# A fused attention and GLU block, forward and backward: GLU LayerNorms moved by one iteration, eight fold products of the backward moved into dQ's bank, start of the backward reordered

## The chip, the cores and the metric

The kernel runs on one core of one Trainium2 chip. The time is the device time of one execution in microseconds (us). A core has five engines that run side by side, each in its own program order: TensorE (PE in the profile, with its weight loads as PEld), VectorE (DVE), ScalarE (ACT), GpSimd (POOL) and SyncE (SP, which here only issues transfers). POOL and ACT issue transfers too. All transfers are carried out by 16 DMA engines. Matrix products write into PSUM, and ACT or DVE copy the results out ("evacuation").

## The reference

One block with two residual branches, and the gradients of all its inputs (cut to what matters):

```python
sa, ca, ga, sb, cb, gb = mod                    # six vectors from silu(c) @ w_mod
h = layernorm(x) * (1 + ca) + sa                # x: 1 x 2048 x 512
x = x + ga * A(h)                               # attention over segments with a memory
h = layernorm(x) * (1 + cb) + sb
x = x + gb * ((sigmoid(h @ w_gate) * (h @ w_up)) @ w_down)     # w_gate, w_up: 512 x 1792

def A(x):                                       # 64 segments of 32 rows, 32 heads of 128
    for s in range(64):
        h = concat([mem, x[32 * s:32 * s + 32]])          # mem: 8 rows, so 40 rows
        q, k, v = h @ Wq, h @ Wk, h @ Wv                  # per head
        p = softmax(where(mask, q @ k.T * scale, -1e9))
        o = (p @ v) @ Wo
        mem = o[:8]                                       # goes on to the next segment
        outs.append(o[8:])

out, vjp = jax.vjp(block, x, mem0, Wq, Wk, Wv, Wo, w_gate, w_up, w_down, c, w_mod)
return out, *vjp(grad_out)
```

Segments hang together through `mem`, forward from first to last, and in the gradient from last to first.

## The kernel before

The work has phases, one after the other: a preparation, the 64 forward segments (phase 2, to about 980 us of the span), the GLU forward and backward (phase 3, 980 to 1318) with its weight gradients (to 1490), the 64 backward segments (phase 4, 1490 to 2479), and the gradients of the attention's weights (phase 5, to the end).

**Phase 2's end.** The probabilities of a segment are transposed on PE and stored in `Pst` by `turn_p` (L872): a copy of rows 96 to 127 and a product with `rden` on rows 0 to 119. For the last segment both are on DVE, in three pieces.

**Phase 3, the GLU.** 16 tiles of 128 rows pass through seven stages, `s0` to `s6`, in a software pipeline of 22 iterations (`run_pipeline`). In iteration `it`, stage k works on tile `it - k`, the deepest stage first, so that `s0` is the last of an iteration. After the stages, `after(it)` runs what else is due.
- `s0(j)` issues the loads of tile j + 1 on SP (four of AOA, then x and grad_out) and makes tile j's residual and LayerNorm: L1150 to L1173, nearly all on DVE; a power on POOL gives `rstd` (L1161), ACT copies the normalised rows to bf16 as `xh2` (L1166, "xh" in the profile, needed in the LayerNorm's backward). Its results are `h2` ("h") and `db`, the gradient of the GLU's output.
- `s1(j)` transposes `h2` and `db` into `hdT` with two DMA transposes on SP (L1183, L1184). Tile 0's LayerNorm and `hdT` are made in phase 2.
- `s2(j)` multiplies by w_gate and w_up (L1205, L1209): 4 groups each of 4 matmuls into 5 PSUM buffers that ACT empties as `sg` (sigmoid, L1206) and `u`. Afterwards DVE makes `hh` and `umh` (L1213, L1215).
- `s3(j)` multiplies `db` by w_down's transpose (L1234); DVE makes `du` and `dg`; SP transposes `hh`, `du` and `dg` (L1227, L1252, L1253), for `s4` to `s6`, which end in L1249 and L1274, the LayerNorm's backward and the stores.

The weights' transposes are made on PE as well, in pieces that `turns` hangs on iterations 2 to 4. `wdT_piece(c)` (L1120) makes two groups of seven transposes of w_down and evacuates each (128 x 896): the first on DVE, the second on ACT. `wT_piece` does the like for w_gate and w_up (L1114, evacuated on ACT, "Wq"). The weights, gradients and transposed weights lie in memory that phases 2 and 4 use under the names Wk, Wv and Wq, and the profile shows those names. PE's and ACT's order is pinned as written up to iteration 2, DVE's order for all of the phase.

**Phase 4, the start.** `ptiles` makes tiles and clears them on POOL (L1562): `dS`, `dOst`, `dKT`, `dQT`, `Qst`, `Kst`. DVE clears `dOT` (L1567). Then SP loads the rows of the last segments, and `proj_b`, twice, multiplies the gradients' rows by Wo's transpose and evacuates them into `RBd`, on ACT and on DVE. `turn_b` transposes RBd, `to_heads` copies the 8 tail rows of each head into dOT on POOL, `dO_tails` (L1675) copies rows of RBd into rows 96 to 119 of `dOst` with three DMAs of POOL (L1678), and one DMA stores zeros of dS as the first gradient of `mem` (L1681). The first `g_ps` product of the first step (L1748) reads dOst.

**Phase 4, a step.** For each segment, `dht` collects the gradient of the segment's input through V's and K's weights in the bank `dh_ps` (128 x 512, four groups of 32 rows that are still to be added). `fold_split` writes it as two bf16 tiles, hi (ACT, L312) and lo (DVE, L313), into the tile dST. `dht_pairs` makes Q's part in a bank `dhq_ps` of 128 x 256 with 16 quads of matmuls (L223), and `split_pair` splits that bank into `dh_hi` (ACT, L230) and `dh_lo` (DVE, L232). `tail.chunk()` then issues some of the products for the 24 or 16 matmuls of the tail rows (`dh_tps`), in all but the first four steps. `fold_sum` (L323) adds it all up: eight products of `dST` with `foldsel`, four of `dh_hi` and four of `dh_lo` with `foldhalf`, into `dh_ft`. ACT copies 8 of its columns into `dyT` (L1866) of the next segment, with which the next step's first products on PE begin. Within phase 4's loop every engine's order is pinned as written.

Of the kernel before, what the change touches and what calls it, by code (L numbers as in the profile page):

```python
# [9 lines left out]
AF = mybir.ActivationFunctionType  # L10
# [30 lines left out]
class K:  # L41
# [395 lines left out]
    def phase2(self):  # L437
        nc, tc, cfg, io = self.nc, self.tc, self.cfg, self.io
        D, DC, H, E, L, M, T, G, NS = cfg.D, cfg.DC, cfg.H, cfg.E, cfg.L, cfg.M, cfg.T, cfg.G, cfg.NS
        GW = 128  # L440
        NP = 3
        PG = 4
# [10 lines left out]
        with ExitStack() as ctx:  # L453
# [39 lines left out]
            NT = cfg.NT  # L493
# [309 lines left out]
            for s in range(NS):  # L803
# [67 lines left out]

                def turn_p(pi):  # L872
                    ps, n = transposes_part(ET, pi)
                    nc.vector.tensor_copy(Pst[96:128, pi * PG:pi * PG + n, :], ps[96:128])
                    nc.vector.tensor_tensor(Pst[0:120, pi * PG:pi * PG + n, :], ps[0:120],
                                            rden[:, pi * PG:pi * PG + n].unsqueeze(2).to_broadcast([120, n, 128]), op=ALU.mult)

# [199 lines left out]
    def phase3(self):  # L1077
# [9 lines left out]
        with ExitStack() as ctx:  # L1087
# [29 lines left out]
                                  tp[:, 0:m * DC, :].rearrange("p (i c) d -> p i (c d)", i=m))  # L1117
                return f

            def wdT_piece(c):  # L1120
                def f():
                    for f0 in range(0, FC, 7):
                        tp = tp8()
                        for i in range(7):
                            nc.tensor.transpose(tp[:, i, :], w_down[:, f0 + i, c * 128:(c + 1) * 128], self.ident[:])
                        self.evac("act" if f0 else "dve", w_downT[:, c, f0 * 128:(f0 + 7) * 128],
                                  tp[:, 0:7, :].rearrange("p i f -> p (i f)"))
                return f

            turns = {2: [wdT_piece(c) for c in range(DC)] + [wT_piece(w_gate, w_gateT, 0, 4, None)],  # L1130
                     3: [wT_piece(w_gate, w_gateT, 4, 10, None), wT_piece(w_up, w_upT, 0, 4, None)],
                     4: [wT_piece(w_up, w_upT, 4, 10, None)]}

# [7 lines left out]
            def s0(j):  # L1141
                r0, r1 = j * 128, (j + 1) * 128
                load(j + 1)
                st = ins.pop(j)
                if j == 0:
                    st.update(x1=self.first_x1, rstd=self.first_st[:, 9:10], xh2=self.first_xh2)
                    return st
                a_rows = st["a_rows"]
                t0 = sbp.tile([128, D], F32, name="t0", tag="f32tmp", bufs=5)
                nc.vector.tensor_tensor(t0[:], a_rows[:], ga_bc[:], op=ALU.mult)  # L1150
                x1 = sbp.tile([128, D], F32, name="x1", bufs=4)
                nc.vector.tensor_tensor(x1[:], t0[:], st["x0"][:], op=ALU.add)
# [12 lines left out]
                nc.vector.tensor_scalar(xhf[:], x1[:], mv[:, 0:1], rstd[:, 0:1], op0=ALU.subtract, op1=ALU.mult)  # L1165
                nc.scalar.activation(xh2[:], xhf[:], AF.Copy)  # L1166
# [3 lines left out]
                nc.vector.tensor_tensor(h2[:], h2a[:], sb_bc[:], op=ALU.add)  # L1170
                nc.gpsimd.dma_start(self.H2ROWS[r0:r1, :], h2[:])
                db = sbp.tile([128, D], BF16, name="db", bufs=2)
                nc.vector.tensor_tensor(db[:], st["dout"][:], gb_bc[:], op=ALU.mult)  # L1173
                nc.gpsimd.dma_start(self.DBROWS[r0:r1, :], db[:])
                st.update(db=db, x1=x1, rstd=rstd, xh2=xh2, h2=h2)
                return st

            def s1(j, st):
                if j == 0:
                    st["hdT"] = self.first_hdT  # L1180
                    return st
                hdT = sbp.tile([128, 2 * DC, 128], BF16, name="hdT", bufs=2)
                nc.sync.dma_start(hdT[:, 0:DC, :], st["h2"][:], transpose=True)  # L1183
                nc.sync.dma_start(hdT[:, DC:2 * DC, :], st["db"][:], transpose=True)  # L1184
                st["hdT"] = hdT
                return st
# [7 lines left out]
            def s2(j, st):  # L1194
# [23 lines left out]
                st.update(sg=sg, hh=hh, umh=umh)  # L1218
                if j == NT - 1:
                    last_hh.append(hh)  # L1220
                return st

            def s3(j, st):
# [151 lines left out]
                if it >= 5:  # L1375
                    later(it)

            self.run_pipeline(NT, [s0, s1, s2, s3, s4, s5, s6], deepest_first=True, after=after)
            self.pin(i0, [ET.DVE])
            self.pin_behind(i0, self.pinned, [ET.PE, ET.DVE, ET.Activation, ET.Pool, ET.SP])  # L1380
            accs = self.flat(self.Wk, 2 * DC * F, 2 * D, F32)
# [148 lines left out]
    def phase4(self):  # L1530
# [7 lines left out]
        with self.p4_ctx as ctx:  # L1538
# [29 lines left out]
            RAd = pt.tile([128, 8 * 128], BF16, name="RAd")  # L1568
            RBds = [pt.tile([128, 8 * 128], BF16, name=f"RBd{i}") for i in range(2)]
            btd = pt.tile([128, 8, 128], BF16, name="btd")  # L1570
            dSs = ptiles("dS", 1)
            dSTs = ptiles("dST", 1, zero=False)
            dOst_t = ptiles("dOst", 1)[0]
            dXTs = {nm: ptiles(nm, n, zero=nm != "dVT") for nm, n in (("dVT", 1), ("dKT", 1), ("dQT", 1))}

            def part3(t, pi):
                return t[:, pi * PW:min((pi + 1) * PW, G * GW)].rearrange("p (g x) -> p g x", x=GW)
# [91 lines left out]
            get_loads(NS - 1)  # L1669
            for hf in range(2):  # L1670
                proj_b(NS // 4 - 1, hf)()()
            turn_b(NS // 4 - 1)()
            to_heads("pool", btd[:], 0, 8, 32, 8, 24)

            def dO_tails(s):  # L1675
                for j in range(3):
                    o = 32 * j + 8 * (s % 4)
                    nc.gpsimd.dma_start(dOst_t[96 + 8 * j:104 + 8 * j, 0:1024], RBds[(s // 4) % 2][o:o + 8, :])  # L1678

            dO_tails(NS - 1)  # L1680
            nc.gpsimd.dma_start(self.DHA[NS, 0:M, :], dSs[0][0:M, 0:D])  # L1681
            nseg_t = 128 // T
            row_stores = []

# [7 lines left out]
            for s in reversed(range(NS)):  # L1692
# [88 lines left out]
                def dht_pairs(X, WT):  # L1781
                    ps = psp.tile([128, 256], F32, name="dhq_ps", tag="p")
                    off = lambda h: (h // 3) * GW + (h % 3) * 32
                    for n in range(H // 2):
                        hs = (2 * n, 2 * n + 1)
                        self.pair_mm(ps, [X[:, off(h):off(h) + 32] for h in hs], [WT[:, h, :] for h in hs], n, H // 2)
                    return ps

                for a, n, eng in ((0, 4, "dve"), (4, 2, "act"), (6, 2, "act")):
# [71 lines left out]
                if split:  # L1861
                    self.pop_later()
                store_rows_x(2)
                ft = self.fold_sum(psp, parts, "dh", "p", pair)
                if dyT_next is not None:
                    nc.scalar.activation(dyT_next[:, :, 0:M], ft[:, :, 0:M], AF.Copy)  # L1866
                g = s // 4
# [428 lines left out]
```

## Time and profile before

| what | us |
|---|---|
| runs: median of 3 (lowest, highest) | 3049.66 (3047.43, 3052.71) |
| profiled execution | 3048.13 |
| its span | 3046.3 |
| busy: PE, DVE, ACT, POOL | 2965.3, 1604.1, 1286.8, 1220.3 |
| granted TensorE clock, mean | 0.993 |
| one step of phase 4 | about 15 |
| one iteration of phase 3, in its middle | 18.8 |

The span runs from the first to the last instruction that the profile holds; times of events below are counted from its start. In lists of events, a row has the start, the duration, the engine, the line of the kernel, the operation, what it writes and reads with the shapes, how many in a row are gathered in it, and in brackets the idle time of the engine just before it with what ended that idle time. "SPq" is SP's queue of transfers; "PEld" a weight load, which runs beside PE's products. Where a row gathers several instructions, its duration goes from the first one's start to the last one's end. Matmuls overlap, so that the price of one is read from start to start.

### The profile page before, as it was taken

Reading aid. Unit: us, or ns where it says so; the run is one execution under the profiler, and the core shown is the slowest. Engines: PE = TensorE matmul, PEld = TensorE weight load, DVE = VectorE, ACT = ScalarE, POOL = GpSimd, SP = SyncE. Lnnn points to the kernel's source line nnn. Section 1 sums busy time; section 2 is a strip of 40 time slices with the busy share of each in tenths; the row PEclk is TensorE's granted clock in tenths of the full one; section 3 lists DMA queues with packets and bytes.
Section 4 is the critical chain, followed back from the end, with each engine's and each line's share of the span. In section 5 each row is a group of like instructions: output and inputs, shape, how many; then the busy total and the mean of one; then the engine's idle time right before and its main releaser. Section 6 shows DMA issues by size and latency. Waiting matters only on the chain.

```text
span 3046.3 us, 106520 instructions
## 1 busy us (share of the span) xinstructions
PE 2965.3 (97%) x44223; PEld 1858.1 (61%) x44297; DVE 1604.1 (53%) x3744; ACT 1286.8 (42%) x3182; POOL 1220.3 (40%) x2645
## 2 busy tenths in 40 slices
PE   6999999999998999999899999999999999999999
PEld 3666666666665544446577777777777754445454
DVE  5656656656655788723355555555555532222221
ACT  2555555555554544312355555555555521101111
POOL 2555555555555222211344444444444422333321
PEclk8999999999999999999999999999999999999999
DMA  9888888888889899987699999999999997666574
GB/s 303 219 224 203 210 220 213 211 213 217 214 209 277 197 232 228 234 267 256 193 249 246 245 244 245 247 248 245 245 247 248 246 288 255 220 196 219 176 241 148
DMA packets 838439, 703.44 MB, mean 231 GB/s; under 512 B 538722, under 2 KB 710914, under 8 KB 837060
## 3 DMA queue, kind: packets, MB, share of 16 engines
q1 hardware_dynamic: 710852, 485.11, 64.0%
q0 software_dynamic: 54512, 148.63, 15.5%
q10 hardware_dynamic: 72592, 62.89, 6.6%
q8 instruction: 348, 5.70, 0.8%
q14 instruction: 135, 1.11, 0.1%
HBM read 295.09 MB, written 276.35 MB: 188 GB/s over the span
## 4 chain that ended last, share of the span: by engine, by line
PE 44%; issue 4%; DMA 1%; POOL 1%; SPq 0%; DVE 0%; ACT 0%; ACTq 0%; POOLq 0%
PE gps L2086 9%; PE dh_ps L215 8%; PE g_ps L1748 6%; PE pass_ps L255 5%; PE gps5o L2100 4%; PE dhq_ps L223 4%; PE dh_tps L215 3%; PE dp_ps L1725 2%; PE tps L1658 2%; PE dp_ps L1733 1%; PE turn_ps L1612 1%; PE dh_ft L323 1%; POOL out_dram L2090 1%; DMA rows<-DVR 1%; DMA rows<-OSR 0%
## 5 line engine op out<-in xcount | busy, mean ns | idle before, releaser
L2086 PE MATMUL gps<-rows,hrows 128*128 128x512 bf16 (+2 forms) x2124 | 415.6, 355 | 1.9
L2086 PEld LDWEIGHTS <-hrows 128*128 128x128 bf16 x2160 | 211.2, 98 | 204.6
L61 ACT ACTIVATE ot<-gps 128x512 bf16<-128x512 f32 (+3 forms) x75 | 41.3, 551 | 376.7 <-PE gps L2086 224.8
L1792 POOL COPY dOst<-RAd 96x512 bf16<-96x512 bf16 x128 | 75.3, 611 | 307.1 <-DVE RAd L63 306.6
L63 DVE CAST ot<-gps 128x512 bf16<-128x512 f32 (+3 forms) x76 | 48.2, 634 | 277.8 <-PE gps L2086 194.4
L658 PE MATMUL pass_ps<-Wv,hT 128*32 128x512 bf16 (+2 forms) x2304 | 188.2, 357 | 0.0
L2090 POOL DMA_DIRECT2D out_dram<-ot x108 | 81.4, 753 | 261.1 <-DVE ot L63 134.3
L255 PEld LDWEIGHTS <-hT 128*32 128x32 bf16 x4096 | 125.2, 97 | 94.4 <-DMA Wq<-in_A_Wq_dram 4.5
L1034 POOL TENSOR_TENSOR Pst<-Pst,rden 120x1408 bf16<-120x1408 bf16 x63 | 159.8, 2536 | 50.2 <-issue 33.8
L61 ACT ACTIVATE dVT<-g_ps 128x480 bf16<-128x480 f32 (+1 forms) x192 | 104.7, 545 | 95.4 <-PE g_ps L1748 95.1
L63 DVE CAST Vst<-pass_ps 96x512 bf16<-96x512 f32 x128 | 87.3, 682 | 106.4 <-ACT RBv L61 101.5
L215 PE MATMUL dh_ps<-WvT,dVT 128*32 128x512 bf16 x2048 | 133.4, 380 | 0.1
L255 PE MATMUL pass_ps<-Wq,hT 128*32 128x512 bf16 x2048 | 125.6, 383 | 4.3 <-DMA Wq<-in_A_Wq_dram 4.3
L2100 PE MATMUL gps5o<-WoT,rows 128*128 128x512 bf16 x580 | 127.8, 379 | 1.0 <-DMA rows<-OSR 0.3
L223 PE MATMUL at_ps<-Wo,OT 128*32 128x256 bf16 x4096 | 125.4, 275 | 3.0 <-DMA Wo<-in_A_Wo_dram 2.6
L658 PE MATMUL pass_ps<-Wv,hb 128*32 128x512 bf16 (+2 forms) x636 | 127.2, 345 | 0.0
L255 PE MATMUL pass_ps<-Wk,hT 128*32 128x512 bf16 x2048 | 125.2, 382 | 1.7 <-POOL hT L547 1.1
L255 PE MATMUL pass_ps<-WoT,dyT 128*32 128x256 bf16 (+1 forms) x3072 | 122.4, 308 | 0.9 <-ACT dyT L1866 0.9
L793 POOL DMA_DIRECT2D Vst<-RBv x192 | 99.2, 522 | 59.4 <-ACT ET L840 38.5
L223 PE MATMUL dhq_ps<-WqT,dQT 128*32 128x256 bf16 x4096 | 122.9, 273 | 0.0
L215 PE MATMUL dh_ps<-WkT,dKT 128*32 128x512 bf16 x2048 | 122.3, 380 | 0.0
L223 PEld LDWEIGHTS <-dQT 128*32 128x32 bf16 x4096 | 109.9, 97 | 15.5
(450 smaller groups left out, 6988.1 us busy)
## 6 DMA issues: line engine op xcount, KB each, us to landing
OSR<-Ost SPq DMA_DIRECT2D x64, 352.0 KB
OT<-OT SPq DMA_DIRECT2D x64, 352.0 KB
VT<-VTr SPq DMA_DIRECT2D x64, 352.0 KB
PS<-Pst SPq DMA_DIRECT2D x64, 352.0 KB
OT_l<-OT SPq DMA_DIRECT2D x64, 352.0 KB
Pst_l<-PS SPq DMA_DIRECT2D x64, 352.0 KB
VT_l<-VT SPq DMA_DIRECT2D x64, 352.0 KB
DVR<-rows_x POOLq DMA_DIRECT2D x64, 352.0 KB, 5.8
```

Source lines behind the costliest of these rows:

```text
L61: return nc.scalar.activation(out, in_, AF.Copy)
L63: return nc.vector.tensor_copy(out, in_)
L215: self.nc.tensor.matmul(ps[32 * j:32 * j + 32, :], lhsT=lhsT, rhs=w, start=(n < 4), stop=(n >= total - 4), tile_position=(0, 32 * j))
L223: nc.tensor.matmul(ps[32 * j:32 * j + 32, :], lhsT=x[k], rhs=w[k][:, 256 * d:256 * d + 256], start=(n == 0), stop=(n == total - 1), tile_p ...
L255: self.nc.tensor.matmul(ps[32 * j:32 * j + 32, :], lhsT=lhs(c), rhs=rhs, start=(c == 0), stop=(c == DC - 1), tile_position=(0, 32 * j))
L658: nc.tensor.matmul(ps[32 * j:32 * j + 32, o * E:(o + n) * E], lhsT=lhsT, rhs=wc[:, 3 * a + hl:3 * (a + n - 1) + hl + 1:3, :], start=(c == ...
L793: nc.gpsimd.dma_start(Vst[96 + 8 * j:104 + 8 * j, :], rb[32 * j + o:32 * j + o + 8, :])
L1034: nc.gpsimd.tensor_tensor(Pst[0:120, :, :], Pst[0:120, :, :], rden[:, :].unsqueeze(2).to_broadcast([120, G, 128]), op=ALU.mult)
L1748: nc.tensor.matmul(ps[:, j, 0:w], lhsT=lh[:, g * GW:(g + 1) * GW], rhs=rh[:, g * GW:g * GW + w], start=True, stop=True)
L2086: nc.tensor.matmul(ps[:, 0:ng * E], lhsT=hrows[:, tp_, c * 128:(c + 1) * 128], rhs=rows[:, tp_, 0:ng * E], start=(tp_ == 0), stop=(tp_ == ...
L2090: nc.gpsimd.dma_start(outw[c * 128:(c + 1) * 128, h0:h0 + 3 * (ng - 1) + 1:3, :], ot[:, 0:ng * E].rearrange("p (h e) -> p h e", e=E))
L2100: nc.tensor.matmul(pss[gg][:], lhsT=src[0][:, src[1], gg * E:(gg + 1) * E], rhs=dyrows[:, tp_, :], start=(tp_ == order[0]), stop=(tp_ == o ...
```

## The change

```diff
 def turn_p(pi):
-    nc.vector.tensor_copy(Pst[96:128, pi * PG:pi * PG + n, :], ps[96:128])
+    nc.scalar.activation(Pst[96:128, pi * PG:pi * PG + n, :], ps[96:128], AF.Copy)
...
-def wdT_piece(c):
-    def f():
-        for f0 in range(0, FC, 7):
+def wdT_pieces():
+    for f0 in range(0, FC, 7):
+        for c in range(DC):
             tp = tp8()
             for i in range(7):
                 nc.tensor.transpose(tp[:, i, :], w_down[:, f0 + i, c * 128:(c + 1) * 128], self.ident[:])
-            self.evac("act" if f0 else "dve", w_downT[:, c, f0 * 128:(f0 + 7) * 128],
+            self.evac("dve" if f0 else "act", w_downT[:, c, f0 * 128:(f0 + 7) * 128],
                       tp[:, 0:7, :].rearrange("p i f -> p (i f)"))
-turns = {2: [wdT_piece(c) for c in range(DC)] + [wT_piece(w_gate, w_gateT, 0, 4, None)],
+turns = {2: [wT_piece(w_gate, w_gateT, 0, 4, None)],
...
 # s0(j)
-nc.scalar.activation(xh2[:], xhf[:], AF.Copy)
+if j == 1:
+    nc.gpsimd.tensor_copy(xh2[:], xhf[:])
+else:
+    nc.scalar.activation(xh2[:], xhf[:], AF.Copy)
...
 # s1(j)
+if j == 1:
+    tp = tp8()
+    for i in range(2 * DC):
+        src = st["h2"] if i < DC else st["db"]
+        nc.tensor.transpose(tp[:, i, :], src[:, (i % DC) * 128:(i % DC) * 128 + 128], self.ident[:])
+    nc.scalar.activation(hdT[:], tp[:], AF.Copy)
+    st["hdT"] = hdT
+    return st
...
 # end of s2(j)
+if j == 0:
+    wdT_pieces()
...
-self.run_pipeline(NT, [s0, s1, s2, s3, s4, s5, s6], deepest_first=True, after=after)
+first = lambda j: s0(j) if j < 2 else None
+second = lambda j, st: s1(j, st if j < 2 else s0(j))
+self.run_pipeline(NT, [first, second, s2, s3, s4, s5, s6], deepest_first=True, after=after)
...
 # phase 4, before the loop
-dSs = ptiles("dS", 1)
+dSs = ptiles("dS", 1, zero=False)
-dOst_t = ptiles("dOst", 1)[0]
-dXTs = {nm: ptiles(nm, n, zero=nm != "dVT") for nm, n in (("dVT", 1), ("dKT", 1), ("dQT", 1))}
+dOst_t = ptiles("dOst", 1, zero=False)[0]
+nc.vector.memset(dOst_t[:], 0.0)
+dXTs = {nm: ptiles(nm, n, zero=False) for nm, n in (("dVT", 1), ("dKT", 1), ("dQT", 1))}
+nc.vector.memset(dSs[0][0:32, 0:D], 0.0)
+for t in (dSs[0], dXTs["dKT"][0], dXTs["dQT"][0]):
+    nc.vector.memset(t[:].rearrange("p (g x) -> p g x", x=GW)[:, :, 120:GW], 0.0)
...
-turn_b(NS // 4 - 1)()
-to_heads("pool", btd[:], 0, 8, 32, 8, 24)
...
+i0 = len(self.traced())
 dO_tails(NS - 1)
+turn_b(NS // 4 - 1)()
+to_heads("pool", btd[:], 0, 8, 32, 8, 24)
 nc.gpsimd.dma_start(self.DHA[NS, 0:M, :], dSs[0][0:M, 0:D])
+self.pin(i0, [mybir.EngineType.Pool])
...
 # dht_pairs, every step of phase 4
-    self.pair_mm(ps, [...], [...], n, H // 2)
+    self.pair_mm(ps, [...], [...], n, H // 2 + 1)
+self.pair_mm(ps, [self.foldsel[:, :]] * 2, parts, H // 2, H // 2 + 1)
...
-ft = self.fold_sum(psp, parts, "dh", "p", pair)
+ft = self.sum_pair(psp, pair, "dh", "p")
```

In words:
- At phase 2's end, the copies of 32 rows go to ACT.
- In phase 3 the LayerNorm of tiles 2 to 15 is made one iteration later, directly before `s1` of the same tile. Tiles 0 and 1 keep their place. Tile 1's `xh2` is copied on POOL, and its `hdT` is made by eight transposes on PE and one copy on ACT, in place of two DMA transposes. The eight groups of w_down's transposes come directly after tile 0's `s2`, the first four evacuated on ACT, the last four on DVE.
- At phase 4's start, POOL clears only Qst and Kst. DVE clears dOst, and of dS, dKT and dQT only the pad columns (120 to 127 of each of 11 groups), and of dS also the rows that are stored as zeros. The three DMAs of `dO_tails` come first on POOL, and POOL's order there is pinned.
- In each step, hi and lo of V's and K's bank are no longer folded by eight products of `fold_sum`. One more quad of `pair_mm`, with `foldsel` as the weights, adds them into Q's bank before that one is split, and `sum_pair` (unchanged; it was used elsewhere) makes the eight remaining products:

```python
def sum_pair(self, psp, parts, name, tag):
    ft = psp.tile([128, self.cfg.DC, 32], F32, name=name + "_ft", tag=tag)
    for i in range(2):
        for c in range(self.cfg.DC):
            self.nc.tensor.matmul(ft[:, c, :], lhsT=parts[i][:, (c % 2) * 128:(c % 2) * 128 + 128],
                                  rhs=self.foldhalf[:, c // 2, :], start=(i == 0 and c == 0), stop=(i == 1),
                                  skip_group_check=True)
    return ft
```

More of the change, by code (lines that the diff above doesn't have):

```diff
@@ L1125, in f @@
                             nc.tensor.transpose(tp[:, i, :], w_down[:, f0 + i, c * 128:(c + 1) * 128], self.ident[:])
-                        self.evac("act" if f0 else "dve", w_downT[:, c, f0 * 128:(f0 + 7) * 128],
+                        self.evac("dve" if f0 else "act", w_downT[:, c, f0 * 128:(f0 + 7) * 128],
                                   tp[:, 0:7, :].rearrange("p i f -> p (i f)"))
-                return f
-            turns = {2: [wdT_piece(c) for c in range(DC)] + [wT_piece(w_gate, w_gateT, 0, 4, None)],
+            turns = {2: [wT_piece(w_gate, w_gateT, 0, 4, None)],
                      3: [wT_piece(w_gate, w_gateT, 4, 10, None), wT_piece(w_up, w_upT, 0, 4, None)],
@@ L1785, in dht_pairs @@
                         hs = (2 * n, 2 * n + 1)
-                        self.pair_mm(ps, [X[:, off(h):off(h) + 32] for h in hs], [WT[:, h, :] for h in hs], n, H // 2)
+                        self.pair_mm(ps, [X[:, off(h):off(h) + 32] for h in hs], [WT[:, h, :] for h in hs], n, H // 2 + 1)
+                    self.pair_mm(ps, [self.foldsel[:, :]] * 2, parts, H // 2, H // 2 + 1)
                     return ps
```

## The prediction

> **What bounds the kernel now.** I read the page's first part, then windows of the places the diff touches, then the timeline of each, and last the waits of PE in the stretches that repeat. Page and windows (columns of a window: us; busy and instruction count of PE, PEld, DVE, ACT, POOL; granted clock; DMA share; GB/s):
>
> ```profile
> PE 2965.3 (97%) x44223; PEld 1858.1 (61%) x44297; DVE 1604.1 (53%) x3744; ACT 1286.8 (42%) x3182; POOL 1220.3 (40%) x2645
> ...
> 988.00:1004.00 16.00, 13.68 (x104) 8.75 (x103) 11.76 (x21) 9.08 (x14) 3.36 (x6) 0.79 0.61 173
> 1004.00:1290.00 286.00, 279.46 (x1503) 137.36 (x1517) 232.87 (x420) 118.75 (x201) 68.19 (x125) 1.00 0.96 224
> 1490.00:1505.00 15.00, 6.95 (x110) 3.87 (x108) 5.28 (x13) 2.71 (x9) 12.18 (x17) 0.85 0.63 202
> 1565.00:2455.00 890.00, 888.48 (x18606) 635.91 (x18610) 516.92 (x1304) 471.38 (x1217) 415.50 (x1027) 1.00 1.00 246
> ```
>
> PE (TensorE) is the bound: 888.48 of 890 us in the backward steps, 279.46 of 286 in the GLU's repeating part, at clock 1.00. So time is won in two ways: fewer PE instructions in those stretches, or the holes at the GLU's start (clock 0.79) and at the backward's start (PE 6.95 of 15, clock 0.85).
>
> **Part 1, the GLU's start.** Timeline (start, duration, engine, line, operation, idle before it and its releaser):
>
> ```profile
> 986.74 0.63 ACT L1166 ACTIVATE xh<-xhf 128x512 bf16<-128x512 f32 x1 [9.85 <-DVE xhf L1165]
> 987.28 0.53 ACT L1206 ACTIVATE sg<-mm 128x448 bf16<-128x448 f32 x1
> 987.86 1.07 PE L1209 MATMUL mm<-Wk,Wq 128*128 128x448 bf16 x4 [4.28 <-ACT sg L1206]
> ...
> 994.45 0.55 PE L1125 MATMUL tp<-ident,Wv 128*128 128x128 bf16 x7 [1.70 <-ACT w_downT L61]
> ...
> 1003.31 0.92 PE L1205 MATMUL mm<-Wk,hdT 128*128 128x448 bf16 x4
> ```
>
> ACT runs in order: tile 1's xh waits for its LayerNorm on DVE and stands ahead of tile 0's first sigmoid, so PE, with its five PSUM buffers full, idles 4.28 us; the clock then reads 0.62, 0.53 (988 to 992). Next, LayerNorm 2 occupies DVE from 989.16 to 994.98, ahead of its w_downT copies. s2(1), PE's next long block, starts at 1003.31.
>
> After: xh(1) is on POOL, so ACT is free. PE fills five buffers by 979.63 + 5 x 0.757 (one L1205 group) = 983.4. The first evacuations must outwait the stores that last read sg's and u's memory. I put the second of these at 984.8, where SP issues a request that waits on the same lane. PE then idles about 1 us and s2(0) ends near 986.8 instead of 991.71. Up to s2(1) PE has 64 transposes (56 of w_down, 8 added for hdT(1)), 7 of them 0.46 apart: 4.2 us; 16 of w_gate, 0.9; 16 matmuls L1234 of 0.19, 3.05. That gives 995.0. With 0.6 for the chain of eight copies (four on ACT at 0.92, four on DVE at 0.62) and hdT's own (1.0): 995.6, 7.7 us earlier. LayerNorm 2 (5.8 us) now stands on DVE behind hh, du, dg of tile 0, as LayerNorm 3 does before: there dg ends at 1005.60 and ACT's Wq copies, queued behind the LayerNorm's xh, come at 1010.71, 5.1 later. After, dg ends 7.7 earlier at best, nearer 6.4 as DVE first makes four of the w_downT copies: 1004.3 for the Wq copies. So 6.4 remain, and **I take 6.2**. Lower bound 4 (stores land 1 us later, one more 1 us copy wait); upper 8.5 (7.7, plus the 0.72 that PE waits for ACT's Wq at 1011.78). POOL's copy of xh(1) has no row: between L1792's 0.61 and L1034's 2.5. It is needed only in tile 1's backward, over 30 us on; its cost is nothing, and at 2.5 it would delay only the H2ROWS store.
>
> The same move in each later tile: LayerNorm keeps its slot on DVE, but hdT's two transposes now follow it at once, and on SP stand behind AOA, x and DAOT and ahead of duT, dgT, hhT.
>
> ```profile
> 1107.34 0.38 SPq L1325 DMA_DIRECT2D DAOT<-daT  x1
> 1108.95 1.72 SPq L1252 DMA_TRANSPOSE duT<-du  x1
> ...
> 1107.89 0.69 DVE L1170 TENSOR_TENSOR h<-h2a,Wv 128x512 bf16<-128x512 f32 x1
> ...
> 1117.82 0.92 PE L1205 MATMUL mm<-Wk,hdT 128*128 128x448 bf16 x4
> ...
> 1109.00:1110.00 1.00, 1.00 (x6) 0.46 (x5) 1.00 (x2) 0.00 (x0) 0.97 (x2) 1.00 0.08 16
> ```
>
> h is ready at 1108.58; hdT(h) takes SP 1.2 to 1.3, so it is issued by 1109.9 and needed by s2 at 1117.82: 7.9 us, where it had 16. The db half is needed only one iteration later. duT, issued to 1110.67 now, moves to about 1112.7 to 1114 (db's transpose takes 2.2 to 2.5) and is needed at 1124.54; dgT and hhT follow, needed 3 and 6 us after it. SP is busy 15 of 18.8 us in either order. The DMA engines, 0.96 busy on average, run empty just then (share 0.08), so I cost it at 0; the cover is those 7.9 us. The slowest landing I find is duT in the tail, issue ended 1282.98, used 1290.59: 7.6. The tail's own wait (3.36 us) stays.
>
> At phase 2's end three copies leave DVE (1.22 us) for ACT: up to 0.3 us, hidden by the stores above; 0.
>
> **Part 2, the backward's start.**
>
> ```profile
> 1497.61 1.29 POOL L1562 MEMSET Kst<- 128x1408 bf16 x1
> 1498.83 1.17 POOL L65 COPY dOT<-btd 128x192 bf16<-128x192 bf16 x4
> 1499.95 1.57 POOL L1678 DMA_DIRECT2D dOst<-RBd  x3
> ...
> 1504.33 0.56 PE L1748 MATMUL g_ps<-Pst_l,dOst 128*128 128x120 bf16 x4 [6.83 <-DMA dOst<-RBd]
> ```
>
> POOL does six memsets of 1.2 to 1.3, then the copies, then the three tail DMAs for which PE waits. After: two memsets, the rest on DVE, idle from 1492.32 to 1493.73: dOst some 0.65 (dOT's took 0.61), a quarter of dS and three pads 0.1 to 0.2 each by their sizes, to 1493.7. With 0.2 more, RBd's cast slips by 0.2. The tail DMAs wait for that cast (1493.73 + 0.69) and issue 1494.5 to 1496.1. They took 2.6 us from the last issue's end to PE's release (1501.52 to 1504.13), so they land at 1498.7. The copies queued behind them, 1.17 + 0.52 + 0.61, end at 1498.4. In front of them six loads of 352 KB are still moving (share over 0.9 to 1498), and SP's Qst and Kst loads (1497.71, 1498.92), which wait for the two memsets left, join some 4 us sooner: up to 1 us later. PE starts at 1498.8 to 1499.8, 4.5 to 5.5 earlier. Its gap shrinks to 1.3 to 2.3 us. The clock, 0.50 when PE resumed, stays up: the 3.36 us gap at 1290 left 1.00. The block up to 1507.57 takes 3.24 us here and 2.12 in a later step (1716.02 to 1718.14): 1.1 more. **I take 5.8**; 3.5 (landing slow, clock lost) to 6.7.
>
> The Trainium skill ("DMA: Bandwidth & Descriptors", section "Anatomy of one DMA") puts a GpSimd DMA's fixed cost at about 2.0 us plus bytes, less than this trace's 2.6. By it the tails land at 1498.1 and the gain would be nearer 6.5; the sum uses the row.
>
> **Part 3, the fold, 64 times.** Per step eight fold products go from the end, and one quad of 128x256 is added to dQ's bank before it is split into hi and lo.
>
> ```profile
> 1787.17 0.38 ACT L230 ACTIVATE dh_hi<-dhq_ps 128x256 bf16<-128x256 f32 x1 [1.09 <-PE dhq_ps L223]
> 1787.59 0.42 DVE L232 TENSOR_TENSOR dh_lo<-dhq_ps,dh_hi 128x256 bf16<-128x256 f32 x1 [0.78 <-ACT dh_hi L230]
> ...
> 1787.92 0.36 PE L323 MATMUL dh_ft<-foldsel,dST 128*128 128x32 bf16 x8
> ...
> 1788.13 0.25 PE L323 MATMUL dh_ft<-foldsel,dh_hi 128*128 128x32 bf16 x4
> ...
> 1788.23 0.25 PE L323 MATMUL dh_ft<-foldsel,dh_lo 128*128 128x32 bf16 x4
> ```
>
> Removed: 1788.13 - 1787.92 = 0.21. Added: four at 27 ns (48 of L223 from 1770.28 to 1771.59) = 0.11. So 0.10 net, if lo is ready. It ends at 1788.01 and is used at 1788.23: 0.22 of slack. Split 0.11 later it ends at 1788.12, while PE would want it at 1788.13; with a semaphore's 0.05, such a step saves 0.055. These are half of the steps with tail pieces; in the other half (lo ends 1772.65, used 1773.31) the full 0.10. In the first four steps PE already waits on dh_hi and dh_lo (0.2 each), so the quad's 0.11 is lost. 30 x 0.10 + 30 x 0.055 - 4 x 0.11 = **4.2**. The dST split (DVE, to 1771.45) ends about 0.2 before the quad would start; with that cover gone every step could lose up to 0.11. Bounds: -3 to 6.5 (0.10 in all).
>
> **Sum.** 6.2 + 5.8 + 4.2 = 16.2 off the profiled execution's 3048.13 (span 3046.3): 3031.9. The median of the runs is 1.5 above it: 3033.4.
>
> **Rivals.**
> 1. The fold gives nothing or less: lo, or the dST split, is last in every step. For: 0.22 and 0.2 us are all the margins. Against: slack of 0.22 in half of the steps, 0.66 in the others. 4.2 lost plus up to 3: 3037.6 to 3040.6. Chance 0.13.
> 2. The GLU's gain is given back: evacuations wait for the stores, or LayerNorm 2 comes late to s2(2). For: DMA share 0.86 to 0.92 at 980 to 986. Against: PE has 8 us of work before it needs w_downT. 2 instead of 6.2: 3037.6. Chance 0.13.
> 3. Slower: hdT(h) becomes the last wait in the repeating GLU. It decides once landing takes more than 7.9 us after issue; being 2.4 us late (10.3) costs 14 x 2.4 = 33.6 us, giving 3067; being 1.6 late brings it to 3055.8. For: average DMA share 0.96, one landing of 7.6. Against: that one lay among 1.4 MB of loads, and here the engines run empty. Chance 0.08.
> 4. PE's gap at 1498 stays, since the loads or another input land last: 5.8 lost, 3039.2. Chance 0.06. For: six loads end near 1500. Against: PE named only dOst.
>
> **How the numbers follow.** The forecast, 3033.4, has 0.60. Its own parts span some 3029 to 3039; 3027 to 3043 takes in rivals 1, 2 and 4 and leaves out the slower one and pairs of failures. 0.2% of 3049.66 is 6.1 us, about what can be told from no change. Faster, under 3043.6: forecast and most of rivals 1, 2, 4, 0.85. Same 0.07, where two of these meet. Slower 0.08.
>
> **What would show it.** Right: no PE wait over 2 us between 980 and 1012, clock 1.00 there, s2(1) about 7 us earlier; first g_ps some 5 us sooner against the phase's start, clock 1.00; steps 0.05 to 0.10 shorter than 15 us. Wrong: PE L1205 waiting for DMA hdT in every iteration, PE L323 waiting over 0.1 us for dh_lo in most steps, or a wait for loads of Pst_l, VT_l at the backward's start.

## The result and the profile after

| | before | changed |
|---|---|---|
| median of 5 runs each, us | 3049.66 (3044.62 to 3052.71) | 3037.14 (3034.76 to 3041.11) |
| ratio, 95% interval | | 0.9962 (0.9951 to 0.9973) |
| span of the profiled execution, us | 3046.3 | 3035.4 |
| mean granted clock | 0.993 | 0.995 |

The change makes the kernel faster by 0.4%: 11.6 us by the ratio, 8.2 to 14.9 by its interval. The forecast was 3033.4, with 3027 to 3043 as its range. So the sign and the range held, and the gain was some 5 us smaller than the 16.2 of the sum. One of the three terms failed almost wholly, as the parts below show. All ratios are of fast runs; one of e2's nine executions took 5350.12 us at a granted clock of 0.761 and is left out of its ratio.

The page's first part, and windows of the stretches that answer to those shown of before (us; busy and instruction count of PE, PEld, DVE, ACT, POOL; granted clock; DMA share; GB/s):

```profile
PE 2958.5 (97%) x43975; PEld 1852.1 (61%) x44049; DVE 1605.5 (53%) x3746; ACT 1290.0 (42%) x3185; POOL 1219.8 (40%) x2642
...
980.00:996.00 16.00, 11.96 (x117) 7.95 (x116) 10.38 (x17) 9.71 (x15) 4.98 (x9) 1.00 0.60 199
996.00:1282.00 286.00, 280.00 (x1505) 137.50 (x1520) 238.75 (x432) 119.77 (x203) 70.14 (x128) 1.00 0.92 228
1482.40:1497.40 15.00, 8.39 (x123) 5.32 (x122) 6.72 (x18) 3.21 (x9) 7.55 (x14) 0.90 0.69 203
1557.70:2444.00 886.30, 884.83 (x18366) 631.50 (x18366) 517.21 (x1303) 471.80 (x1217) 416.88 (x1027) 1.00 1.00 247
```

The GLU's start now has clock 1.00 (0.79 before) in this trace; in six of the other traces with the new GLU (e1, e2, e4, e5, e6, e8) the clock still fell there, for 3.4 us at a time. The backward's start is hardly better: PE 8.39 of 15 us at clock 0.90, against 6.95 at 0.85. The repeating parts are as dense as they were.

One trace must not be compared with one other trace as a whole. In the changed kernel's trace phase 2 reaches the last segment's `at_ps` products at 966.71 instead of 968.98, before any changed line has run (the first, the copy into `Pst`, starts at 970.7); in other traces they come anywhere from 965.9 to 973.4. The time before is therefore cut into stretches that start at an event of the kernel itself. Three of them hold the change:

| stretch, us | kernels without the part | kernels with it | gain | forecast |
|---|---|---|---|---|
| last at_ps to the first product of the GLU's fourth s2 block | 73.6, 74.2 | 67.5, 65.6, 66.6, 66.2, 69.0, 71.1, 67.4 | 6.3 | 6.2 |
| first product of phase 4 to the first dyT copy | 26.3, 27.1, 26.7, 26.7 | 26.3, 25.8, 24.7, 24.5, 25.2, 25.6 | 1.4 | 5.8 |
| first dyT copy to the last | 937.6, 938.3 | 934.2 to 935.3 (11 traces) | 3.3 | 4.2 |

Each number is one trace (before, changed kernel, and the experiments that leave that part alone), each gain a difference of means. They add up to 11.0, within the interval of the runs. A fourth stretch, from the sixteenth s2 block to the first product of phase 4, has no term in the forecast: it took 222.6 us in the two traces with the old GLU and 220.4 to 225.3, 223.6 in the mean, in the eleven with the new one. That may take back 1.0 us, but it is less than the scatter.

**The GLU's start.** Timeline of the changed kernel (start, duration, engine, line, operation, idle before it and its releaser):

```profile
983.44 0.54 ACT L1216 ACTIVATE sg<-mm 128x448 bf16<-128x448 f32 x1 [8.34 <-DMA Wv<-AOA]
...
984.04 0.92 PE L1219 MATMUL mm<-Wk,Wq 128*128 128x448 bf16 x4 [3.02 <-ACT sg L1216]
...
988.32 0.55 PE L1125 MATMUL tp<-ident,Wv 128*128 128x128 bf16 x7 [0.97 <-ACT w_downT L61]
...
995.51 0.92 PE L1215 MATMUL mm<-Wk,hdT 128*128 128x448 bf16 x4
...
1004.36 0.61 PE L1114 MATMUL tp<-ident,Wk 128*128 128x128 bf16 x8 [0.87 <-ACT Wq L61]
...
1012.81 0.36 PE L1215 MATMUL mm<-Wk,hdT 128*128 128x448 bf16 x1 [0.51 <-DMA hdT<-h]
```

ACT no longer stands behind tile 1's LayerNorm: sg's copy waits for a DMA to land, and PE waits for sg 3.02 us instead of 4.28. s2(1) starts at 995.51 and Wq's copies end PE's next wait at 1004.36, where the forecast had 995.6 and 1004.3. The agreement is partly chance: PE begins the GLU 2.56 us earlier here than in the trace of before, and the wait of about 1 us that was forecast is 3.02. PE's early start alone is not the reason: in e4, e5 and e7 to e10 it begins the GLU just as early (976.2 to 978.2), and this wait is 1.2 to 1.7. Why the landing is late in this one trace stays open. A new, small wait is the last line: tile 2's hdT.

**The repeating GLU.** DVE makes h, SP transposes it, and the last line is the s2 block that reads it:

```profile
1099.49 0.69 DVE L1172 TENSOR_TENSOR h<-h2a,Wv 128x512 bf16<-128x512 f32 x1
...
1100.24 1.21 SPq L1193 DMA_TRANSPOSE hdT<-h  x1
1101.54 1.21 SPq L1194 DMA_TRANSPOSE hdT<-db  x1
...
1109.42 0.92 PE L1215 MATMUL mm<-Wk,hdT 128*128 128x448 bf16 x4
```

hdT(h) is issued by 1101.45, eight us ahead of its use, and PE waits for nothing there. From the fourth to the sixteenth s2 block all 13 traces take 225.65 or 225.66 us: the moved LayerNorm costs nothing.

**The backward's start.** POOL and PE, the chain of waits (its row begins with start and us), and windows of the clock:

```profile
1485.15 1.29 POOL L1576 MEMSET Kst<- 128x1408 bf16 x1
1487.39 1.58 POOL L1694 DMA_DIRECT2D dOst<-RBd  x3 [0.94 <-ACT btd L61]
...
1495.28 0.56 PE L1768 MATMUL g_ps<-Pst_l,dOst 128*128 128x120 bf16 x4 [5.40 <-DMA dOst<-RBd]
...
1488.44 6.64 DMA dOst<-RBd
...
1494.00:1496.00 2.00, 0.72 (x8) 0.75 (x9) 0.00 (x0) 0.12 (x1) 0.00 (x0) 0.57 0.50 177
1498.00:1500.00 2.00, 2.00 (x24) 1.01 (x26) 1.66 (x3) 0.65 (x2) 0.26 (x2) 0.50 0.03 8
1500.00:1502.00 2.00, 2.00 (x30) 1.00 (x23) 0.00 (x0) 0.37 (x1) 0.00 (x0) 0.73 0.00 0
```

Phase 4 starts 7.62 us earlier in this trace than before. On that scale the tails are issued 4.9 us sooner (5.4 forecast), and PE still waits 5.40 us for them. They landed at 1495.08 (1488.44 + 6.64), 6.1 us after the last issue's end at 1488.97, where 2.6 had been assumed. The clock went to 0.50 at 1494.3 and stayed there for 6.8 us, 5.8 of them after PE had resumed; before, it was also 6.8 us, of which only 3.0 fell on PE's work. Half of that difference, 1.4 us, is what PE lost again.

**The fold.** A step with 16 tail matmuls at its end:

```profile
1778.79 0.28 PE L223 MATMUL dhq_ps<-dST,foldsel 128*32 128x256 bf16 x4
1779.12 0.38 ACT L230 ACTIVATE dh_hi<-dhq_ps 128x256 bf16<-128x256 f32 x1 [1.20 <-PE dhq_ps L223]
1779.54 0.43 DVE L232 TENSOR_TENSOR dh_lo<-dhq_ps,dh_hi 128x256 bf16<-128x256 f32 x1 [0.89 <-ACT dh_hi L230]
...
1779.86 0.27 PE L240 MATMUL dh_ft<-foldsel,dh_hi 128*128 128x32 bf16 x4
...
1780.02 0.27 PE L240 MATMUL dh_ft<-foldsel,dh_lo 128*128 128x32 bf16 x4
```

lo ends at 1779.97, and its products start at 1780.02, 0.16 after hi's instead of 0.10: lo is now the last wait in these steps, as forecast. The quad takes 0.11 on PE (start to the next product).

### The profile page after: what moved, and what is told of

Same layout as the page of the kernel before. It is cut to its first block, busy times and chain, and to the rows that moved or that the text cites. A ratio compares the mean times of both kernels' runs of the same rounds, so it can differ in the third digit from the quotient of the medians.

```text
span 3035.4 us, 106027 instructions
## 1 busy us (share of the span) xinstructions
PE 2958.5 (97%) x43975; PEld 1852.1 (61%) x44049; DVE 1605.5 (53%) x3746; ACT 1290.0 (42%) x3185; POOL 1219.8 (40%) x2642
## 4 chain that ended last, share of the span: by engine, by line
PE 89%; DMA 4%; issue 3%; DVE 2%; ACT 1%; POOL 1%; SPq 0%; another core or an unknown queue 0%; DVEq 0%; POOLq 0%; ACTq 0%
PE pass_ps L255 14%; PE gps L2107 11%; PE dh_ps L215 8%; PE g_ps L1768 6%; PE pass_ps L658 5%; PE gps5o L2121 4%; PE dhq_ps L223 4%; PE at_ps L223 4%; PE gps L1444 3%; PE mm L1286 3%; PE dh_tps L215 3%; PE turn_ps L828 2%; PE dp_ps L1745 2%; PE tps L1676 2%; PE mm L1261 1%
```

## The experiments

Theory after the first traces: the tail DMAs are held up on the DMA engines by the 352 KB loads queued there, and the other two parts do what was forecast. The main rival: a GpSimd DMA of so few rows is slow by itself. The first four kernels test this and take the parts one by one; the next six test the theory again and take the GLU's part apart; the last is a control.

**e1, the second segment's loads held until the tails are issued.**

```diff
 def get_loads(s, held=False):
...
+    if held:
+        nc.gpsimd.memset(t[0:32, 0:8], 0.0)
     nc.sync.dma_start(gl3(t), dram[s])
...
 dO_tails(NS - 1)
+get_loads(NS - 2, held=True)
```

> The changed kernel, but the three 352 KB loads of the second backward segment are issued only after the three tail DMAs (a 32x8 memset on POOL, behind those DMAs, is what they wait for). Theory: in the changed kernel the tails were issued 7.6 us sooner as forecast, but landed 6.64 us after the last issue (before: 2.6) because eight loads of 352 KB were queued on the same DMA engines. With three loads out of the way the tails should land within about 3 us, PE should wait under 3 us at the phase's start instead of 5.40, the clock should stay at 1.00 there, and the stretch from the phase's first product to the first dyT copy should shrink from 26.3 us to 20 to 22.5; in all 4 to 6 us off the changed kernel. Rival: a GpSimd DMA of 8 rows simply takes 5 to 7 us when issued there; then the wait stays over 5 us and the stretch within 0.5 us of 26.3.

The chain of waits of e1, and PE's wait:

```profile
1489.78 5.96 DMA dOst<-RBd
...
1495.94 0.37 PE L1773 MATMUL g_ps<-Pst_l,dOst 128*128 128x120 bf16 x4 [4.71 <-DMA dOst<-RBd]
```

The wait was 4.71 us and the stretch 24.4: between the theory's 20 to 22.5 and the rival's 26.3, so it decides nothing. (Two numbers of the expectation are on another scale than its 2.6 us: the 7.6 us are the earlier start of phase 4 itself, and the 6.64 us count from the last issue's start. The tails were issued 4.9 us sooner against the phase's start and landed 6.1 us after the last issue's end.) The loads had gone out again 0.7 us behind the tails (1490.44), and the tails' 24 packets of 2 KB ran among them from 1491.2 to 1493.8. Ratio to before 0.9958 (0.9945 to 0.9971).

**e2, the start of the backward undone.** The changed kernel with the first lines of phase 4 as in before (the part's diff, reversed):

```diff
-dSs = ptiles("dS", 1, zero=False)
+dSs = ptiles("dS", 1)
...
+turn_b(NS // 4 - 1)()
+to_heads("pool", btd[:], 0, 8, 32, 8, 24)
...
 dO_tails(NS - 1)
-turn_b(NS // 4 - 1)()
-to_heads("pool", btd[:], 0, 8, 32, 8, 24)
```

> The changed kernel with the start of the backward as it was before (six memsets on POOL, tail DMAs after the copies). Theory: that part brought nothing, since the tails waited for the loads either way and the clock gave back the 1.4 us won; the stretch from the phase's first product to the first dyT copy is 26.3 us in both kernels, so this one should run within 0.5 us of the changed kernel there and in its whole span, apart from what phase 2 varies by. Rival (my forecast): 5.8 us slower than the changed kernel.

The stretch is 26.7 us against 26.3 and 25.8 in two traces of the changed kernel; the ratio is 0.9971 (0.9961 to 0.9981) against 0.9962. My 5.8 us are refuted; half a microsecond to one and a half is what the part is worth.

**e3, the fold alone**, on the kernel before:

```diff
+self.pair_mm(ps, [self.foldsel[:, :]] * 2, parts, H // 2, H // 2 + 1)
...
-ft = self.fold_sum(psp, parts, "dh", "p", pair)
+ft = self.sum_pair(psp, pair, "dh", "p")
```

> The kernel before with the fold change alone. Theory: the three intervals between dyT copies of the first steps grow by 0.11 us each, the other 59 shrink by 0.03 to 0.04 (steps with 16 tail matmuls at their end) or 0.08 to 0.09 (the rest), in all 3.3 us less from the first dyT copy to the last; nothing else moves. Rival (forecast): 4.2.

The first three intervals took 44.49 us instead of 44.16 (0.11 each), the other 59 took 890.39 instead of 893.40: 2.7 less in all, in the one trace. A cycle of four steps takes 14.89, 14.91, 15.03, 15.55 instead of 14.92, 14.95, 15.12, 15.64, in e3 as in the changed kernel.

**e4, phases 2 and 3 alone.** e2 with the fold undone as well:

```diff
-self.pair_mm(ps, [self.foldsel[:, :]] * 2, parts, H // 2, H // 2 + 1)
...
-ft = self.sum_pair(psp, pair, "dh", "p")
+ft = self.fold_sum(psp, parts, "dh", "p", pair)
```

> The kernel before with the changes of phases 2 and 3 alone. Theory: from the GLU's first product to its fourth s2 block it gains 5.9 us as in the changed kernel, and 5.2 to 5.9 to the first product of the backward, depending on whether the wait for duT in the tail makes the clock drop. Rival: the 5.9 partly came from what phase 2 varied by (2.3 us earlier in that one trace, before any changed line), then it differs by up to 2 us.

From its first GLU product to the fourth s2 block it took 58.6 us, before 63.0, the changed kernel 57.1; from the last at_ps 69.0 (before 73.6 and 74.2). That is 4.4 gained, 1.5 less than in the changed kernel, which is the rival's number but not its reason: at_ps came at 966.94 here, within 0.3 us of the changed kernel's trace. PE waited 2.2 us for tile 0's hhT, a DMA transpose, which the changed kernel's traces do not show. To the first product of the backward 3.6 us are gained, below the 5.2 to 5.9 expected.

**e5, everything but three loads held until the tails have landed.**

```diff
-load_rows(Qst_t, self.QST, NS - 1)
-load_rows(Kst_t, self.KST, NS - 1)
...
 dO_tails(NS - 1)
+landed = pt.tile([24, 8], BF16, name="landed")
+nc.sync.dma_start(landed[:], dOst_t[96:120, 0:8])
+load_rows(Qst_t, self.QST, NS - 1)
+load_rows(Kst_t, self.KST, NS - 1)
+get_loads(NS - 2)
+self.pin(i1, [mybir.EngineType.SP])
```

> The changed kernel, but SP issues only the first segment's three loads (OT, Pst, VT) before the tails; Qst, Kst and the second segment's three loads wait until the tails have landed (a 24x8 transfer of dOst's tail rows that SP issues in front of them waits for the landing). In e1 the loads went out again 0.7 us after the tails and the tails' packets still ran among them, for 5.96 us. Theory (packets of the loads hold the tails up on the shared DMA engines): with 1.06 MB done before the tails are issued, these land within 2.6 to 3.5 us of the last issue, PE waits 0.5 to 2 us instead of 5.40, the clock stays at 1.00, and the stretch from the phase's first product to the first dyT copy is 20 to 22 us (changed kernel 26.3, e1 24.4), unless the late Qst or Kst adds a wait of 1 to 2 us. Rival (the tails are slow by themselves): landing 5.5 us or more after the issue, stretch over 24 us.

PE's first g_ps in e5:

```profile
1494.06 0.37 PE L1773 MATMUL g_ps<-Pst_l,dOst 128*128 128x120 bf16 x4 [1.75 <-POOL dOst L1818]
```

The releaser is now POOL's copy and no longer the DMA: with the engines free the tails' packets ran from 1490.92 to 1492.18, right behind their issue (1489.80 to 1491.38). SP's request that waits for their landing went out at 1493.97, 2.6 us after the last issue's end, as the release did in the kernel before; POOL's copy ended at the same time. The clock stayed at 1.00 and the stretch is 21.3 us: the theory's number. 0.54 and 0.70 us are lost again to Qst and Kst. The tails are issued at the same place on the phase's scale as in the changed kernel (4.1 us after its first product), so they are not slow by themselves: the loads in the queues held them up. Ratio 0.9953 (0.9939 to 0.9968).

This trace also shows the largest wait of the GLU's start, which no line of e5 touches:

```profile
1005.45 0.61 PE L1261 MATMUL mm<-Wv,hhT 128*128 128x512 bf16 x1 [4.76 <-DMA hhT<-hh]
```

It was 0 in the changed kernel's two traces, 0.5 in e2, 2.2 in e4 and 2.5 in e10. It is absent in e1 and e6 to e9, and in the two traces with the old GLU.

**e6, xh2 of tile 1 on ACT again:**

```diff
-if j == 1:
-    nc.gpsimd.tensor_copy(xh2[:], xhf[:])
-else:
-    nc.scalar.activation(xh2[:], xhf[:], AF.Copy)
+nc.scalar.activation(xh2[:], xhf[:], AF.Copy)
```

> The changed kernel with xh2 of tile 1 copied on ACT again. Theory: ACT's first sigmoid waits behind this copy, which waits for tile 1's LayerNorm; it starts 2 to 3 us later after the last segment's at_ps products than in the changed kernel (13.5 to 16.7 us there in four runs, 18 to 19 before), and that delay goes through to the fourth s2 block: 69 to 70.5 us from at_ps instead of 66.2 to 69. Rival: the chain is held by DVE and SP anyway, then the fourth s2 block is where it was.

```profile
985.61 0.63 ACT L1165 ACTIVATE xh<-xhf 128x512 bf16<-128x512 f32 x1 [9.57 <-DVE xhf L1164]
986.15 0.53 ACT L1213 ACTIVATE sg<-mm 128x448 bf16<-128x448 f32 x1
...
986.72 0.92 PE L1216 MATMUL mm<-Wk,Wq 128*128 128x448 bf16 x4 [3.22 <-ACT sg L1213]
```

sg came 18.5 us after the last at_ps and the fourth s2 block 70.2 after it (mean with the copy on POOL: 67.6), as the theory has it. The copy on POOL is worth some 2.6 us by this, but the kernels that have it scatter from 65.6 to 71.1, so that its worth at the fourth block is not shown; the earlier sg is (13.5 to 16.7 us in those).

**e7, LayerNorm of tile 2 at its old place:**

```diff
-first = lambda j: s0(j) if j < 2 else None
-second = lambda j, st: s1(j, st if j < 2 else s0(j))
+first = lambda j: s0(j) if j < 3 else None
+second = lambda j, st: s1(j, st if j < 3 else s0(j))
```

> The changed kernel with the LayerNorm of tile 2 one iteration earlier again, as before. Theory: its 5.8 us on DVE stand between the w_downT copies and hh, du of tile 0; the second s2 block starts as in the changed kernel, but PE runs out of buffers in it and the third s2 block comes 4 to 6 us later than in the changed kernel (17.3 to 17.9 us from the second), of which 1 is given back at the Wq copies. Rival: DVE waits for w_downT's transposes anyway, and LayerNorm 2 fits in between: within 1 us.

The third s2 block came 18.76 us after the second, 0.9 to 1.5 later than the range expected of the changed kernel and not 4 to 6, and inside the 17.3 to 21.8 of the seven traces with its GLU; the fourth came 68.4 after at_ps, inside the scatter. So the theory's size fell, but its mechanism is in the trace:

```profile
996.78 0.63 ACT L1168 ACTIVATE xh<-xhf 128x512 bf16<-128x512 f32 x1 [2.68 <-DVE xhf L1164]
...
998.72 1.08 DVE L1223 TENSOR_TENSOR hh<-sg,u 128x1792 bf16<-128x1792 bf16 x1
...
998.38 0.61 PE L1114 MATMUL tp<-ident,Wk 128*128 128x128 bf16 x8 [2.10 <-ACT Wq L61]
```

LayerNorm 2 runs on DVE right behind the w_downT copies, from 992.98 on, and tile 0's hh starts at 998.72 instead of 993.14 in the changed kernel. ACT's xh waits for it, Wq's copies stand behind xh, and PE waits 2.10 us for them; in the changed kernel its longest such wait is 0.87. So LayerNorm 2 does not fit into DVE's waits, as the rival had it. Most of its delay is made up again up to the third block; by what was not taken apart. Only tile 2 was tried.

**e8, hdT of tile 1 by DMA transposes:**

```diff
-if j == 1:
-    tp = tp8()
...
-    nc.scalar.activation(hdT[:], tp[:], AF.Copy)
-    st["hdT"] = hdT
-    return st
 nc.sync.dma_start(hdT[:, 0:DC, :], st["h2"][:], transpose=True)
```

> The changed kernel with hdT of tile 1 made by the two DMA transposes again. Theory: on SP they stand behind twelve loads of AOA, which went out at 994.9 and 996.8 in the kernel before, and the second s2 block needs h's half at 995.5: it starts 1.5 to 4 us later than in the changed kernel (counted from sg's first copy: 12.1 to 12.4 us there). Rival: the transposes land in time, within 0.5 us.

```profile
994.13 1.24 SPq L1185 DMA_TRANSPOSE hdT<-h  x1
...
996.97 1.67 PE L1207 MATMUL mm<-Wk,hdT 128*128 128x448 bf16 x4 [3.60 <-DMA hdT<-h]
```

The second s2 block started 15.2 us after sg, 2.9 later, with PE waiting 3.60 for it: the theory's number. Counted from at_ps it started at 30.3 us, where the seven traces with the changed GLU have 26.9 to 28.8. At the fourth block 2.0 of it are left (69.6 against 67.6), which is no more than the scatter.

**e9, w_down's transposes at their old place, on DVE and ACT in turn:**

```diff
+turns = {2: [wdT_piece(c) for c in range(DC)] + [wT_piece(w_gate, w_gateT, 0, 4, None)],
-turns = {2: [wT_piece(w_gate, w_gateT, 0, 4, None)],
...
-if j == 0:
-    wdT_pieces()
```

> The changed kernel with w_down's transposes again at the end of iteration 2 (behind tile 1's hdT), evacuated by DVE and ACT in turn. Theory: with DVE free of LayerNorm 2 the order and the engines of these copies matter little, since copies on two engines in turn need less time than four on ACT and then four on DVE; the second s2 block starts 12 to 13 us after sg's first copy (12.1 to 12.4 in the changed kernel). Rival: the earlier place is what shortens the chain; then it starts 1.5 us or more later, 13.9 or above.

The second s2 block started 13.98 us after sg, past the rival's 13.9 by a hair. But e1, whose GLU is the changed kernel's, has 14.4 there, and counted from at_ps e9's 28.9 stands beside 26.9 to 28.8: this decides nothing. The fourth s2 block came 67.6 us after at_ps, as in the mean of the changed kernels, so that no cost of the old place is seen.

**e10, e5 with Qst among the first loads and DHA's store ahead of the tails:**

```diff
 get_loads(NS - 1)
+load_rows(Qst_t, self.QST, NS - 1)
...
+nc.gpsimd.dma_start(self.DHA[NS, 0:M, :], dSs[0][0:M, 0:D])
 dO_tails(NS - 1)
...
-load_rows(Qst_t, self.QST, NS - 1)
...
-nc.gpsimd.dma_start(self.DHA[NS, 0:M, :], dSs[0][0:M, 0:D])
```

> e5 with Qst's load among the first four and DHA's store issued before the tails, in a wait of POOL. Theory: the first g_ps comes 0.5 us earlier than in e5 (8.4 us after the phase's first product), PE's 0.54 for Qst goes and its 0.70 for Kst stays or shrinks; the stretch to the first dyT copy is 20 to 20.8 us (e5 21.3, changed kernel 26.3), so 5 to 6 us off the changed kernel. Rival: the fourth load is still moving when the tails go out and holds them up again, then 21.3 or more.

The wait and the clock in e10:

```profile
1492.10 0.37 PE L1773 MATMUL g_ps<-Pst_l,dOst 128*128 128x120 bf16 x4 [2.29 <-DMA dOst<-RBd]
...
1492.00:1494.00 2.00, 1.90 (x37) 1.83 (x41) 0.33 (x1) 1.11 (x3) 0.97 (x5) 1.00 0.18 18
```

The stretch is 20.4 us, 5.3 and 5.8 under the two traces of the changed kernel. The first g_ps came 8.9 us after the phase's first product and not 7.9: the tails' packets ran beside the last ones of the four loads, they landed 2.9 us after the last issue's end, and they are the last releaser again. But the waits for Qst and Kst are gone. Median 3034.40, ratio 0.9948 (0.9933 to 0.9964). It has the lowest ratio of all that were timed, but its interval overlaps that of the changed kernel on the same chip; that it is faster is shown by the stretch, not by the medians.

**e11, the changed kernel again, beside e10:**

> The changed kernel as it is, on the same chip as e10. Theory: the same stretches as in its first trace in what is bound by PE (15-us steps, the 225.7 us of the GLU's middle), 26 to 26.8 us for the start of the backward, and several us of scatter in what waits for DMAs: the end of phase 2 and the way from the last at_ps products to the fourth s2 block (66 to 71 us in the kernels with the same GLU). Its median stays 10 to 14 us under the kernel before and 4 to 6 above e10.

Median 3036.96, ratio 0.9958 (0.9943 to 0.9972), 14.7 under the kernel before and 2.6 above e10 (I had said 10 to 14 and 4 to 6; runs of one kernel spread over more than 10 us). The start took 25.8 us, the way to the fourth s2 block 65.6, both just under my ranges.

## Why the prediction was right, and where it was wrong

- **GLU's start: right in size, in part by luck** (6.2; 6.3 in the means, with the 0.3 of phase 2's end in it, which I had costed at nothing). ACT's order, SP's queue and LayerNorm 2 on DVE are links of the chain by the waits in e6, e8 and e7; what each is worth at the end (2.6, 2.0 and 0.8 us) is no larger than the scatter. For the place of w_down's transposes e9 decides nothing. The landing that I put at "about 1 us" of idle time cost 3.02 in the changed kernel's trace and 1.2 to 1.7 in six others. The seven traces scatter over 5.5 us; the largest single piece of that is a wait for a DMA, hhT's 4.76 in e5, which no term of mine had.
- **Moved LayerNorms in the repeating part: right** (0). The window of 7.9 us was never used up; tile 2's hdT alone was late, by 0.5 us (1.1 in e2). The rival that it makes the kernel slower is refuted by the 225.65 us.
- **Fold: right in mechanism, a little large.** 4.2 forecast, 3.3 in the means. The first steps lose 0.11 each in seven of the eleven traces and up to 0.17 in the others. The others save 0.04 and 0.09 where I had 0.055 and 0.10.
- **Start of the backward: wrong.** The step that failed: "They took 2.6 us from the last issue's end to PE's release (1501.52 to 1504.13), so they land at 1498.7", with "up to 1 us later" for the loads. The 2.6 were measured when the loads were nearly through. Issued 4.9 us sooner, the same three DMAs fell into the middle of eight loads, 2.8 MB, and took 5.7 to 6.1 us in the six traces with this start; PE's gap was 5.0 to 5.4 us instead of 1.3 to 2.3. That is the outcome of rival 4, to which I had given 0.06, though not its reason: the tails themselves still landed last. Its argument against, that "PE named only dOst", was no argument, since a transfer can be late because of others that nobody waits for. e5 shows the cause: with the loads out of the way the stretch shrinks to 21.3 us, a gain of 5.4 on the kernels with the old start, which is about the 5.8 that I had forecast.
- **The clock** was to stay up because "the 3.36 us gap at 1290 left 1.00". That was one case, not a rule: see below. It gave back 1.4 us in the changed kernel's trace, where 5.8 us of half clock fell on PE's work; in the others with the same start it was 2.7 to 5.4 us. The stretch of this start goes with that: 24.5 and 24.7 us where it was under 3, 25.2 and 25.6 where it was about 4, 25.8 and 26.3 where it was over 5.
- **The signs.** Of my signs of being right, the clock of 1.00 at the GLU's start and the shorter steps came. A PE wait over 2 us (3.02) was there all the same, s2(1) came 5.5 us earlier counted from at_ps instead of about 7, and the first g_ps 1.4 us sooner instead of some 5. The median stayed in my range because that had room for one term that fails: without the 4.4 us by which the backward's start fell short, the sum gives 3037.8.

## What to carry to other kernels

Here three transfers that were issued 4.9 us earlier landed only 1.4 us earlier, because the DMA engines were busy with loads at that time: take a transfer's duration from a row with the same load, and try holding back the transfers that nobody needs yet (e5, e10). Before a gain is credited to one trace, compare stretches that start at events of the kernel itself, since what waits for DMAs scatters by several microseconds. An engine's queue order (a copy that waits for another engine, ahead of one that PE needs) is cheap to mend: with xh on POOL, sg came 1.8 to 5.0 us earlier after at_ps than in e6.

## What the runs showed of the hardware

From the GLU on, the clock fell to 0.50 for 3.4 or 6.8 us at a time, in all 13 traces, and a gap's length did not decide it. In the GLU's tail, PE's wait for duT:

```profile
1290.59 3.20 PE L1274 MATMUL mm<-Wq,duT 128*128 128x512 bf16 x13 [3.36 <-DMA duT<-du]
```

```profile
1281.84 4.88 PE L1286 MATMUL mm<-Wq,duT 128*128 128x512 bf16 x13 [3.02 <-DMA duT<-du]
```

The first is the kernel before, the second the changed one: a gap of 3.36 left the clock at 1.00 and 13 products took 3.20; one of 3.02 was followed by 3.4 us at 0.50, and they took 4.88. In e4 2.52 us were enough, in e10 2.60 were not. What decided is in the traces: within each of them, all falls of the clock lie whole multiples of 3.413 us apart. These are the windows of that grid around the four gaps, of the kernel before, the changed one, e4 and e10:

```profile
1288.86:1292.27 3.41, 1.63 (x7) 0.80 (x9) 3.35 (x6) 0.00 (x0) 1.01 (x2) 1.00 1.17 313
...
1279.23:1282.64 3.41, 0.75 (x3) 0.41 (x5) 3.38 (x7) 0.00 (x0) 0.00 (x0) 1.00 1.21 335
...
1280.39:1283.81 3.42, 0.84 (x4) 0.41 (x5) 3.38 (x7) 0.00 (x0) 0.01 (x1) 1.00 1.19 312
...
1278.62:1282.03 3.41, 1.50 (x7) 0.73 (x9) 3.38 (x6) 0.00 (x0) 0.12 (x1) 1.00 1.25 266
```

PE was busy for 1.63 and 1.50 us of the windows after which the clock stayed, and for 0.75 and 0.84 us of those after which it fell. Over all windows of this grid at full clock (60 to 3025 us of the 13 traces), the clock fell after each of the 42 in which PE was busy, by the profile, for at most 0.42 of the time, after 8 of the 39 between 0.42 and 0.60, and after none above. So a gap counts by the share of one such window that it takes, and the same gap can fall into one window or be split over two. The Trainium skill's page "TensorE: Matmul & The Clock Gate" (section "What's actually happening") describes an activity window of about 3.4 us that runs freely; the grid agrees with it. Its advice in "Why this matters for your kernels", no gap above some 3 us, is not enough here by the 2.52.

In the changed kernel's trace the packets of the tails ran 1.7 to 5.1 us after their last issue's end (0 to 1.3 in the kernel before), among those of loads that SP had issued on another queue, which ran on to 1495.93. The skill's page "DMA: Bandwidth & Descriptors" (section "Issuing engines are not separate DMA queues") says that DMAs of all issuing engines interleave on the same 16 DMA engines; e5 agrees. The 2.0 us that I cited from it as the fixed cost would have made the miss larger.

The copy of 128x512 from f32 to bf16 took POOL 1.13 us, ACT 0.63.
